# Two rows of a token block in one piece per partition, not four, in a fused gated-attention and MLP-mixer kernel

## The chip, the cores and the metric

The kernel runs on one core of a Trainium2 chip. A core has five engines with queues of their own: TensorE (PE; PEld is its weight loads), VectorE (DVE), ScalarE (ACT), GpSimd (POOL) and SyncE (SP). Work moves between the on-chip memories SBUF and PSUM, and DMA engines bring data from DRAM and transpose it. POOL, SP and ACT issue DMAs. Each engine works through its queue in order and waits on semaphores where an operand is not ready.

The metric is the device time of one execution in microseconds (us). The kernel before took 1173.21 us, the median of four runs (1169.92 to 1176.64).

## The reference

```python
# u, v: (8, 3008, 256)   z: (8, 3008, 64)   all float32
scores = (1 / S) * np.matmul(z, z.transpose(0, 2, 1))        # S = 3008
attn   = np.maximum(scores, 0.0) ** 2
x      = u * np.matmul(attn, v)
xt     = x.transpose(0, 2, 1)
h      = np.maximum(xt @ w_tok1, 0.0) @ w_tok2               # mixes tokens: 3008 -> 256 -> 3008
y      = x + h.transpose(0, 2, 1)
h2     = np.maximum(y @ w_ch1, 0.0) @ w_ch2                  # mixes channels: 256 -> 1536 -> 256
out    = y + h2
```

Every batch is independent of the others. The attention matrix of a batch is symmetric, because queries and keys are the same z.

## The kernel before, in words

Tokens are cut into 24 tiles of 128 (the last holds 64), four tiles to a block of 512: six query blocks (`q`, `NQ` = 6) and six key groups (`g`, `NG` = 6) per batch. Within a block the rows are dealt out to partitions: `rows_of` gives partition p four consecutive rows (4p to 4p+3), so a load moves one piece of four rows for each partition, and tile t of the block holds rows 4p + t. Attention does not mind in which order tokens come, as long as every operand has the same one. The last block holds three full tiles and a half one and is dealt three rows at a time.

**Attention.** `score_run` makes scores for two key tiles at a time. z has 64 channels, so a tile's z takes half of PE's rows; `zT` holds z transposed, doubled in both halves, and two score matmuls run side by side on the halves. PE changes between this mode and 128-row matmuls many times. ScalarE takes ReLU into an `at` buffer (six of them), VectorE squares it (L445), and PE multiplies it with v into two accumulators `acc0`, `acc1` (L533). From batch 1 on, a block above the diagonal is also transposed by SP's DMA queue (`flip`, L492) into an `fl` buffer and used again below the diagonal; the diagonal block itself is made as a triangle (L485). When a query block is complete, `gate` (L628) multiplies the two accumulators by `uT`, the transposed u block, into `xT`, and `turn_x` (L640) transposes that on SP.

**Mixer.** A batch's mixer runs between the attention steps of the next batch. `tok1` (L675) adds up over all six blocks; `tok2` (L692) makes h for one block, and VectorE adds it onto `xT` (L698); `ch1` (L729), an evacuation on ScalarE or VectorE (L742, L744), `ch2` (L771), and a residual add (L784) follow, and SP writes the output rows.

**z and its turns.** For batch 0 z is read as float32 on SP and ACT. Blocks 0 and 1 are doubled on VectorE and turned by PE matmuls with an identity, blocks 2 and 3 by DMA, blocks 4 and 5 by PE inside the attention loop (`turn_late_z`). For later batches POOL loads a `zs` buffer (`load_z`), copies it twice into `zr` (L125; two buffers), and SP transposes `zr` into `zT` (L126), one block at a time.

**Loads.** All loads but the first z are asked for by POOL, which casts to bf16 on the way. POOL also reorders w_tok2: `load_w_tok2` brings a piece into a `ws` buffer, and `order_w_tok2` (L220, L224) copies it into the order in which the tiles hold the tokens. A load waits where its buffer is still in use: u has three `ur` buffers, freed by `turn_u` (L189) on SP.

**The order.** The order of all queues is written by a planner at build time, in plain Python: it keeps a modelled time for each engine (`free`, `pe`), a list of waiting operations with a cost and a latency each (`push`), and a ring of three PSUM slots of two banks (`ring`; tag `ps`), which scores, token-mix, channel-mix and output pieces share. At every step the main loop picks scores, a half of an AV group or a mixer piece, by what the model says is ready. A `Piece` is a mixer step. Loads and turns are hung on attention steps by number (`at_group`), and take their place in POOL's or SP's queue when PE's planned order reaches that step. `release`, `live` and `ROOM` count buffers.

Of the kernel before, what the change touches and what calls it, by code (L numbers as in the profile page):

```python
# [13 lines left out]
P = 128  # L14
# [30 lines left out]
class Piece:  # L45


    def __init__(self, cost, needs, fn, opens=False, closes=False, room=None):
        self.cost, self.needs, self.fn = cost, needs, fn
        self.opens, self.closes, self.room = opens, closes, room  # L50


@with_exitstack
def kernel(
# [23 lines left out]
    NG = KT // GK  # L78
    widths = [min(QW, S - q * QW) for q in range(NQ)]
# [15 lines left out]


# [5 lines left out]
    def rows_of(ap, c):  # L102

        n = full_tiles[c]
        return ap[c * QW:c * QW + n * P, :].rearrange("(p t) d -> p t d", t=n)
# [4 lines left out]
    def load_z(b, c):  # L110
        zs = sb.tile([P, GK, d_qk], BF16, tag="zs", name="zs", bufs=6)
        n = full_tiles[c]
        nc.gpsimd.dma_start(out=zs[:, :n, :], in_=rows_of(z[b], c))
        if n < GK:
            for r in range(2):
                nc.gpsimd.dma_start(
                    out=zs[r * TAIL:(r + 1) * TAIL, n, :], in_=last_rows(z[b]))
        loading(LOAD / 4)
        return zs

    def turn_z(zs, zT, c, engine, tag="zr", bufs=2):


        zr = sb.tile([P, GK, 2, d_qk], BF16, tag=tag, name="zr", bufs=bufs)
        engine.tensor_copy(zr[:], zs.unsqueeze(2).to_broadcast([P, GK, 2, d_qk]))  # L125
        nc.sync.dma_start_transpose(  # L126
            out=zT[:, c * GK:c * GK + GK, :], in_=zr.rearrange("p t h d -> p (t h d)"))

    def first_z(c):
# [4 lines left out]
        queues[c % 2].dma_start(out=zf[:, :n, :], in_=rows_of(z[0], c))  # L134
# [25 lines left out]
    def load_v(b, c):  # L160
# [7 lines left out]
        nc.gpsimd.dma_start(out=vt[:, :n, :], in_=rows_of(v[b], c))  # L168
# [7 lines left out]
    def load_u(b, q):  # L176
        ur = sb.tile([P, QW // P, D], BF16, tag="ur", name="ur", bufs=3)
        n = full_tiles[q]
        nc.gpsimd.dma_start(out=ur[:, :n, :], in_=rows_of(u[b], q))
# [15 lines left out]
    def load_w_tok1(c):  # L195
        n = full_tiles[c]
        nc.gpsimd.dma_start(
            out=w_tok1_sb[:, c * GK:c * GK + n, :], in_=rows_of(moe_w_tok1, c))
# [6 lines left out]
    def load_w_tok2(c):  # L205
        st = sb.tile([P, DT, QW], BF16, tag="h2", name="ws", bufs=ROOM["h2"])
        W = widths[c]
        nc.gpsimd.dma_start(
            out=st[:, :, :W],
            in_=moe_w_tok2.rearrange("(tc t) s -> t tc s", t=P)[:, :, c * QW:c * QW + W])  # L210
        ws[c] = st
        live["h2"] += 1
        loading(LOAD)

    def order_w_tok2(c):
        st = ws.pop(c)
        live["h2"] -= 1
        W, n = widths[c], full_tiles[c]
        for h in range(DT):
            nc.gpsimd.tensor_copy(  # L220
                w_tok2_sb[:, h, c * QW:c * QW + n * P].rearrange("p (t s) -> p t s", s=P),
                st[:, h, :n * P].rearrange("p (s t) -> p t s", t=n))
        if n * P < W:
            nc.gpsimd.tensor_copy(  # L224
                w_tok2_sb[:, :, c * QW + n * P:c * QW + W], st[:, :, n * P:W])

# [15 lines left out]
    zTs, vs, urs, uTs, xTs, xs, ws = {}, {}, {}, {}, {}, {}, {}  # L242
# [9 lines left out]

    LAST = NG - 1

# [40 lines left out]

    LOAD = 1.3
# [84 lines left out]
    def score_run(us, start):  # L381
        slots = sorted((d for d in ring if d.t is not None), key=lambda d: d.t)
        for unit in us:
# [12 lines left out]
            for r, i, c0, c1 in parts(unit):  # L396
                k = g * GK + i
                h = slice(r * d_qk, (r + 1) * d_qk)
                nc.tensor.matmul(  # L399
                    sc[:, r, c0:c1], zT[h, k * P:(k + 1) * P],  # L400
                    zT[h, q * QW + c0:q * QW + c1], start=True, stop=True)
# [41 lines left out]
    def square(unit, view, t):  # L443
# [15 lines left out]
        if flips(b, q, g):  # L459
            uses[0] = 2  # L460
            attn = at.rearrange("p (j i s) -> p i j s", i=GK, s=P)
            done = push("sp", t, 2.45, 6.5, lambda t: flip(b, q, g, at, uses, done),
# [5 lines left out]
    def square_triangle(unit, t):  # L468
# [5 lines left out]
        if pr == 0:  # L474
            for j, busy in ((0, 0.55), (1, 0.4)):
# [3 lines left out]
        done = push("sp", t, 0.3, 5.5, lambda t: blocks.update(  # L479
# [136 lines left out]
    def gate(blk, dh, t):  # L616
# [18 lines left out]
        if dh == DT - 1:  # L635
            push("sp", t, 1.25, 7.5, lambda t: turn_x(b, q, t), first=1)
# [22 lines left out]
    def add_mixer(b):  # L659
# [26 lines left out]
        def tok2(q, end):  # L686
# [9 lines left out]
            def add(t):  # L696
                xT = xTs[b, q]
# [413 lines left out]
```

## Time and profile before

| | |
|---|---|
| median of four runs | 1173.21 us (1169.92 to 1176.64) |
| profiled execution, its own time | 1172.68 us |
| span of the profiled execution | 1170.8 us |
| TensorE | 1159.8 us busy, 7049 matmuls |
| VectorE, ScalarE, GpSimd | 541.3, 521.4, 158.9 us busy |
| share of the 16 DMA engines: SP's queue, POOL's queue | 53.6%, 19.9% |
| DMA packets | 472883, of them 27344 on POOL's queue (32.32 MB) |
| POOL copies: z doubling (L125), w_tok2 order (L220) | 42 of 631 ns; 12 of 522 to 816 ns |
| add after the token mix (L698), 1024 elements | 40 of 1214 ns |

How to read it: a group's busy time is the sum of its instructions' durations, and consecutive ones overlap at their ends, so PE's busy time is more than the time in which it streams columns. Idle time ahead of an instruction is put down to what was ready last. In a timeline line, the first number is the start, the second the length of the merged group, x the count, and the square bracket holds the idle time before it and what ended it. DMA shares are averages over all 16 engines. Rows of 40 digits give the busy share of 40 equal slices in tenths.

### The profile page before, as it was taken

To read this page: it belongs to the slowest core of one execution; us is meant where nothing else is said; L and a number is where in the kernel's file an instruction comes from. 1 tells how busy PE (TensorE), PEld (TensorE's weight loads), DVE (VectorE), ACT (ScalarE), POOL (GpSimd) and SP (SyncE) were. 2 spreads that over 40 slices of the span, in tenths; PEclk is the share of its full clock that TensorE was granted. 3 is DMA by queue.
4 is the path that set the end of the run, shared out by engine and by line. 5 is a ranking of instruction groups with operands and counts; after the bars stand their busy time and mean duration, and the time that the engine had idled before them with its cause. 6 is when DMAs were issued, how large, how long until landed. Compare 5 with 4: busy or idle time off the path is not lost.

```text
span 1170.8 us, 17791 instructions
## 1 busy us (share of the span) xinstructions
PE 1159.8 (99%) x7049; PEld 629.8 (54%) x7049; DVE 541.3 (46%) x819; ACT 521.4 (45%) x650; POOL 158.9 (14%) x328
## 2 busy tenths in 40 slices
PE   9999999999999999999999999999999999999998
PEld 3334554655546555555555655465454655555666
DVE  5785653356432554335634355242542336512544
ACT  7876543344542364343534435344454344513221
POOL 3372001102012100120101210101201000000000
PEclk9999999999999999999999999999999999999999
DMA  9999837797487975896759985698667977532121
GB/s 167 171 162 192 176 97 151 155 190 126 119 168 150 168 140 126 158 169 148 142 129 172 159 159 122 136 189 149 122 142 142 188 143 154 121 97 61 50 81 64
DMA packets 472883, 165.57 MB, mean 141 GB/s; under 512 B 436640, under 2 KB 450528, under 8 KB 472800
## 3 DMA queue, kind: packets, MB, share of 16 engines
q1 hardware_dynamic: 444944, 131.74, 53.6%
q0 software_dynamic: 27344, 32.32, 19.9%
q8 instruction: 55, 0.90, 0.3%
q10 hardware_dynamic: 512, 0.38, 0.1%
q14 instruction: 28, 0.23, 0.1%
HBM read 65.40 MB, written 24.64 MB: 77 GB/s over the span
## 4 chain that ended last, share of the span: by engine, by line
PE 95%; DVE 1%; DMA 1%; ACT 1%; issue 1%; SPq 0%; POOL 0%; ACTq 0%; DVEq 0%
PE acc L533 41%; PE op L771 21%; PE hp L729 21%; PE sc L399 6%; PE a_ps L675 4%; PE h_ps L692 3%; ACT at L437 1%; DVE at L445 1%; DMA zf<-in_z_dram 1%; DMA fl<-at 1%; DMA v_sb<-in_v_dram 0%; DVE xT L698 0%; DVE xT L628 0%; DVE h2pre L744 0%; SPq L134 0%
## 5 line engine op out<-in xcount | busy, mean ns | idle before, releaser
L533 PE MATMUL acc<-at,v_sb 128*128 128x512 bf16 (+3 forms) x1464 | 350.7, 378 | 3.5 <-DVE xT L628 2.7
L533 PEld LDWEIGHTS <-v_sb 128*128 128x128 bf16 (+1 forms) x2304 | 209.4, 97 | 269.0 <-issue 66.9
L742 ACT ACTIVATE h2pre<-hp 128x1024 bf16<-128x1024 f32 (+1 forms) x191 | 191.0, 1006 | 364.5 <-PE hp L729 363.4
L437 ACT ACTIVATE at<-sc 128x1024 bf16<-128x1024 f32 (+1 forms) x284 | 272.0, 1024 | 161.6 <-PE sc L399 156.1
L445 DVE TENSOR_TENSOR at<-at 128x1024 bf16<-128x1024 bf16 (+1 forms) x284 | 200.1, 713 | 177.2 <-ACT at L437 176.7
L729 PE MATMUL hp<-xT,w_ch_sb 128*128 128x512 bf16 (+1 forms) x1152 | 266.8, 375 | 0.0
L771 PE MATMUL op<-w_ch_sb,h2pre 128*128 128x256 bf16 x2208 | 258.4, 273 | 0.3 <-DVE xT L698 0.2
L771 PEld LDWEIGHTS <-h2pre 128*128 128x128 bf16 x2208 | 215.9, 98 | 46.2 <-issue 0.5
L533 PE MATMUL acc<-fl,v_sb 128*128 128x512 bf16 (+1 forms) x840 | 199.9, 371 | 0.0
L729 PEld LDWEIGHTS <-w_ch_sb 128*128 128x128 bf16 x1152 | 112.7, 98 | 126.7 <-issue 0.2
L784 DVE TENSOR_TENSOR res<-op,u_sb 128x512 f32<-128x512 f32 x87 | 60.1, 691 | 206.5 <-PE op L771 206.5
L744 DVE TENSOR_SCALAR h2pre<-hp 128x1024 bf16<-128x1024 f32 (+1 forms) x97 | 117.3, 1209 | 52.4 <-PE hp L729 51.5
L628 DVE TENSOR_TENSOR xT<-acc,uT 128x512 bf16<-128x512 f32 (+1 forms) x96 | 63.2, 665 | 113.8 <-PE acc L533 113.6
L399 PE MATMUL sc<-zT 64*128 64x512 bf16 (+1 forms) x732 | 95.0, 360 | 0.3
L425 ACT ACTIVATE at<-sc 128x512 bf16<-128x512 f32 (+3 forms) x164 | 59.2, 446 | 67.7 <-PE sc L399 67.5
L125 POOL COPY zr<-zs 128x512 bf16<-128x512 bf16 x42 | 26.5, 631 | 400.3 <-DMA zT<-zr 394.4
L473 DVE TENSOR_TENSOR at<-at 128x512 bf16<-128x512 bf16 (+3 forms) x164 | 44.4, 324 | 59.2 <-ACT at L425 59.1
L399 PEld LDWEIGHTS <-zT 64*128 64x128 bf16 x732 | 31.3, 94 | 56.8 <-issue 39.4
L698 DVE TENSOR_TENSOR xT<-xT,h_ps 128x1024 bf16<-128x1024 bf16 (+1 forms) x48 | 55.7, 1192 | 6.4 <-PE h_ps L692 6.3
L168 POOL DMA_DIRECT2D v_sb<-in_v_dram x48 | 25.9, 545 | 145.2 <-PE acc L533 144.3
L675 PE MATMUL a_ps<-x_sb,w_tok_sb 128*128 128x256 bf16 x384 | 44.7, 273 | 0.8 <-ACT at L437 0.8
L692 PE MATMUL h_ps<-w_tok_sb,a_sb 128*128 128x512 bf16 (+1 forms) x192 | 44.5, 375 | 0.1
(43 smaller groups left out, 210.0 us busy)
## 6 DMA issues: line engine op xcount, KB each, us to landing
out_dram<-res SPq DMA_DIRECT2D x87, 256.0 KB, 2.2
v_sb<-in_v_dram POOLq DMA_DIRECT2D x40, 256.0 KB, 4.8
ur<-in_u_dram POOLq DMA_DIRECT2D x40, 256.0 KB, 5.1
zs<-in_z_dram POOLq DMA_DIRECT2D x35, 64.0 KB, 4.6
at<-at SPq DMA_TRANSPOSE x123, 2.4
fl<-at SPq DMA_TRANSPOSE x105, 4.0
v_sb<-in_v_dram POOLq DMA_DIRECT2D x8, 192.0 KB, 6.1
ur<-in_u_dram POOLq DMA_DIRECT2D x8, 192.0 KB, 5.5
```

What stands on the lines that cost most here:

```text
L399: nc.tensor.matmul(sc[:, r, c0:c1], zT[h, k * P:(k + 1) * P], zT[h, q * QW + c0:q * QW + c1], start=True, stop=True)
L437: nc.scalar.activation(view, sv, ACT.Relu, scale=inv_S)
L445: nc.vector.tensor_mul(view, view, view)
L533: nc.tensor.matmul(o, vs[blk.b, g][rows, i, dh * P:(dh + 1) * P], rhs, start=first, stop=stop, skip_group_check=True)
L628: nc.vector.tensor_mul(xT[:, dh, :full * P].rearrange("p (t s) -> p t s", s=P), acc[:, :full * P].rearrange("p (t s) -> p t s", s=P), uT[: ...
L675: nc.tensor.matmul(st["a_ps"][:, th, :], w_tok1_sb[:, k, th * P:(th + 1) * P], x[:, :, i, :], start=(k == 0 and th == 0), stop=(k == KT - ...
L692: nc.tensor.matmul(h[:, dh, :W], st["a"][:, th, dh * P:(dh + 1) * P], w_tok2_sb[:, th, q * QW:q * QW + W], start=(th == 0), stop=(th == 1))
L729: nc.tensor.matmul(hp[:, r, :W], w_ch1_sb[:, dc, cc * P:(cc + 1) * P], xT[:, dc, :W], start=(dc == 0), stop=(dc == DT - 1))
L742: nc.scalar.activation(h2[:, :, :W], hp[:, :, :W], ACT.Relu)
L744: nc.vector.tensor_single_scalar(h2[:, :, :W], hp[:, :, :W], 0.0, AX.max)
L771: nc.tensor.matmul(op[:, i, :], h2, w_ch2_sb[:, cc, :], start=(cc == 0 and (i == 0 or apart)), stop=(cc == CHT - 1), skip_group_check=True)
L784: nc.vector.tensor_add(res.rearrange("p i (h d) -> p i h d", d=P), op.rearrange("p i (h d) -> p i h d", d=P), us[:, :, half * 2:half * 2 + ...
```

## The change

The token order. In a full block a partition now holds two pieces of two consecutive rows: tile 2a + t holds rows 256a + 2p + t. `fetch_rows` loads both pieces with one DMA, `out_rows` writes one half of a block as one run of two rows per partition. The last block stays dealt by three.

Along with that:

- w_tok2 is loaded straight into its place in its natural column order (no `ws` buffer, no copies on POOL). The add after the token mix takes h from PSUM at a step of two elements, in two instructions per full block.
- z of batches 1 to 7 goes into one standing tile `zs` with a slot of zeros at either end. One transpose turns pairs of neighbouring tiles: with two transposes shifted by one tile against each other, slot k of `zT` holds tile k-1 in its lower and tile k in its upper rows. So nothing is doubled on POOL; the two halves of a score matmul read slots k+1 and k (`z_tile`). Five transposes per batch, two of six tiles for each half of the batch and one of a single tile.
- z blocks 4 and 5 of batch 0 and the first u block are turned on PE as mixer pieces marked `urgent`; u(0,0) no longer uses a DMA transpose. Its evacuation from PSUM is a VectorE copy of 1024 elements.
- In batch 0 `turn_x` waits until the planned time 62 us; z of batch 1 is loaded from the seventh attention step on, not the nineteenth, and turned in two halves.
- In the planner, a flip costs 1.8 us of SP's time in place of 2.45, each transpose of a triangle 1.2 in place of 0.55, 0.4 and 0.3, and scores may be held back (`together`) until the half tile at the end of the keys can go with them in the same PE mode.

```diff
+    zs = consts.tile([P, KT + 2, d_qk], BF16)
-    def rows_of(ap, c):
-        n = full_tiles[c]
-        return ap[c * QW:c * QW + n * P, :].rearrange("(p t) d -> p t d", t=n)
+    def fetch_rows(queue, to, ap, c):
+        n = full_tiles[c]
+        rows = ap[c * QW:c * QW + n * P, :]
+        if n == GK:
+            queue.dma_start(
+                out=to.rearrange("p (a t) d -> p a t d", a=2),
+                in_=rows.rearrange("(a p t) d -> p a t d", a=2, t=2))
+        else:
+            queue.dma_start(out=to, in_=rows.rearrange("(p t) d -> p t d", t=n))
+    def out_rows(b, q, half):
+        if full_tiles[q] == GK:
+            rows = out[b][q * QW + half * 2 * P:q * QW + (half + 1) * 2 * P, :]
+            return rows.rearrange("(p t) d -> p t d", t=2)
...
-    def turn_z(zs, zT, c, engine, tag="zr", bufs=2):
-        zr = sb.tile([P, GK, 2, d_qk], BF16, tag=tag, name="zr", bufs=bufs)
-        engine.tensor_copy(zr[:], zs.unsqueeze(2).to_broadcast([P, GK, 2, d_qk]))
-        nc.sync.dma_start_transpose(
-            out=zT[:, c * GK:c * GK + GK, :], in_=zr.rearrange("p t h d -> p (t h d)"))
+    def turn_z(zT, half):
+        n = KT // 2
+        for k in (half * n, half * n + 1):
+            nc.sync.dma_start_transpose(
+                out=zT[:, k:k + n:2, :],
+                in_=zs[:, k:k + n, :].rearrange("p t d -> p (t d)"))
+        if half:
+            nc.sync.dma_start_transpose(
+                out=zT[:, KT, :], in_=zs[:, KT:, :].rearrange("p t d -> p (t d)"))
...
     def load_w_tok2(c):
-        st = sb.tile([P, DT, QW], BF16, tag="h2", name="ws", bufs=ROOM["h2"])
+        cols = slice(c * QW, c * QW + widths[c])
         nc.gpsimd.dma_start(
-            out=st[:, :, :W],
-            in_=moe_w_tok2.rearrange("(tc t) s -> t tc s", t=P)[:, :, c * QW:c * QW + W])
+            out=w_tok2_sb[:, :, cols],
+            in_=moe_w_tok2.rearrange("(tc t) s -> t tc s", t=P)[:, :, cols])
-    def order_w_tok2(c):
...
-            done = push("sp", t, 2.45, 6.5, lambda t: flip(b, q, g, at, uses, done),
+            done = push("sp", t, 1.8, 6.5, lambda t: flip(b, q, g, at, uses, done),
...
-            push("sp", t, 1.25, 7.5, lambda t: turn_x(b, q, t), first=1)
+            push("sp", t if b else max(t, LOADED), 1.25, 7.5,
+                 lambda t: turn_x(b, q, t), first=1)
...
             def add(t):
                 xT = xTs[b, q]
-                nc.vector.tensor_add(xT[:, :, :W], xT[:, :, :W], h[:, :, :W])
+                n = full_tiles[q]
+                if n == GK:
+                    to = xT.rearrange("p h (a t s) -> p h a t s", a=2, t=2)
+                    own = h.rearrange("p h (a s t) -> p h a t s", a=2, t=2)
+                    for half in range(2):
+                        nc.vector.tensor_add(
+                            to[:, :, half], to[:, :, half], own[:, :, half])
+                else:
+                    to = xT[:, :, :n * P].rearrange("p h (t s) -> p h t s", t=n)
+                    nc.vector.tensor_add(
+                        to, to, h[:, :, :n * P].rearrange("p h (s t) -> p h t s", t=n))
...
+            at_group(base + NG, lambda b=b: new_zT(b + 1))
             for j, c in enumerate(vorder):
+                ask = base + (NG if b == 0 else 3 * NG - 2)
+                at_group(ask + j, lambda b=b, j=j: load_z(b + 1, j))
+                if j % 3 == 2:
+                    at_group(ask + (2 * j + 4 if b == 0 else j + 3),
+                             lambda b=b, j=j: turn_next_z(b, j // 3))
...
+    def first_u(landed):
+        ur = urs.pop((0, 0))
+        def turn(end):
+            take_slot()
+            up = psum.tile([P, QW // P * DT, P], F32, tag="ps", name="up", bufs=3)
+            for i in range(QW // P * DT):
+                t, h = divmod(i, DT)
+                nc.tensor.matmul(
+                    up[:, i, :], ur[:, t, h * P:(h + 1) * P], ident[:],
+                    start=(i % 4 == 0), stop=True, skip_group_check=True)
+            ring.append(push("dve", end + 0.2, 1.15, 1.3, lambda t: evacuate(up)))
...
+        heads.append(Piece(0.45, [Done(landed)], turn, urgent=True))
...
+    late_z(4, 7.8)
+    late_z(5, 9.0)
+    first_u(18.5)
...
+        together = (
+            blk is not None and blk.q > 1 and blk.b < B - 1 and not blk.tails
+            and blk.slot == 0 and t + 0.3 < tails_ready(blk) < FAR)
+        if n_now and not together and ts <= t + NOW and (whole or (low and n_now >= 2)):
             pick = "scores"
...
+        elif tm <= t + NOW and pieces[0].urgent:
+            pick = "mixer"
```

## The prediction, made before the result was known

> **What bounds the kernel now.** I read the page's busy table and the rows by slice first, then the chain, then the timeline around each place where TensorE stood idle.
>
> ```profile
> PE 1159.8 (99%) x7049; PEld 629.8 (54%) x7049; DVE 541.3 (46%) x819; ACT 521.4 (45%) x650; POOL 158.9 (14%) x328
> ...
> PEclk9999999999999999999999999999999999999999
> DMA  9999837797487975896759985698667977532121
> ...
> PE 95%; DVE 1%; DMA 1%; ACT 1%; issue 1%; SPq 0%; POOL 0%; ACTq 0%; DVEq 0%
> ```
>
> TensorE is the bound at full granted clock, and the chain is TensorE for 95%. A busy PE row overstates matmuls, so I redid it by rate: in the chain 12 AV matmuls of 512 columns take 2.59 us (0.216 each) and 48 of 256 columns 5.24 us (0.109). All matmuls at these rates (scores two at a time, as they run on two row halves) come to 1135 us of the 1170.8 us span. The other 36 us are: about 23 us in 254 changes between 64-row scores and 128-row matmuls (0.09 each, counted in PE's order), about 6 before and after the first and last matmul, and the rest in a few holes, all before 111 us but one. From 120 to 1080 us no 20 us stretch lost more than 0.2 us apart from the changes. So a gain can come from the holes alone, and they are these.
>
> ```profile
> 71.51 9.65 DVE L445 TENSOR_TENSOR at<-at 128x1024 bf16<-128x1024 bf16 x8 [0.76 <-ACT at L437]
> ...
> 74.35 1.91 POOL L220 COPY w_tok_sb<-ws 128x512 bf16<-128x512 bf16 x2
> ...
> 81.81 2.43 PE L533 MATMUL acc<-at,v_sb 128*128 128x448 bf16 x12 [1.29 <-DVE xT L628]
> ```
>
> Eight squares take 9.65 us, 1.2 apiece, while POOL reorders w_tok2 (L220); at 94 us four took 2.55, 0.64 apiece. The gate is late, and PE waits 1.29 us.
>
> ```profile
> 98.60 0.53 POOL L179 DMA_DIRECT2D ur<-in_u_dram  x1 [12.47 <-DMA uT<-ur]
> 99.12 1.08 POOL L113 DMA_DIRECT2D zs<-in_z_dram  x2
> 100.18 8.01 SPq L492 DMA_TRANSPOSE fl<-at  x3
> ...
> 106.29 2.85 ACT L437 ACTIVATE at<-sc 128x1024 bf16<-128x1024 f32 x3 [4.41 <-DMA fl<-at]
> 107.37 1.03 PE L675 MATMUL a_ps<-x_sb,w_tok_sb 128*128 128x256 bf16 x8 [0.80 <-ACT at L437]
> ...
> 109.61 0.37 PE L533 MATMUL acc<-at,v_sb 64*128 64x512 bf16 x1 [1.21 <-DVE xT L628]
> ```
>
> Batch 1's first flips (the transposed copies fl) queue behind late loads; ScalarE cannot overwrite at for 4.41 us, and PE loses 0.80 + 1.21 + 0.22 us.
>
> ```profile
> 11.80 1.04 PE L533 MATMUL acc<-at,v_sb 128*128 128x512 bf16 x4 [0.48 <-DMA v_sb<-in_v_dram]
> ...
> 1094.44 5.52 PE L692 MATMUL h_ps<-w_tok_sb,a_sb 128*128 128x512 bf16 x24
> 1095.51 6.74 DVE L698 TENSOR_TENSOR xT<-xT,h_ps 128x1024 bf16<-128x1024 bf16 x6 [0.46 <-PE h_ps L692]
> 1100.17 3.00 PE L771 MATMUL op<-w_ch_sb,h2pre 128*128 128x256 bf16 x26 [0.21 <-DVE xT L698]
> ```
>
> At 11.8 us PE waits for the second v block. At 1095 us six token-mix pieces outrun six adds (1.12 us apart); three PSUM slots hold them up by 0.64 us in all.
>
> **The change, part by part.**
>
> 1. **w_tok2 reorder and z doubling leave POOL.** 13 copies (L220/L224, 0.5 to 0.8 us) and 42 (L125, 0.63) go; nothing waits for POOL instead, and w_tok2 lands in its place. Squares fall back from 1.2 to 0.64 us, so the wait at 81.8 goes: bounds -1.4 and 0 (if ScalarE, at 0.92 us a pair, were late next). I take **-1.3**.
>
> 2. **Loads earlier, four x turns later.** POOL was held by z copies waiting for z turns (8.3 us at 60), so the w_tok2 and w_ch loads came at 61 to 85 and were still running at 93. Now POOL's queue is v, u, z, w without these waits; batch 0's x turns are moved on SP behind the u and z turns to 62 us and are needed only at about 106. SP's next uses are u turns needed at each gate, 10 us or more later. What is late next is the fifth u load and the four flips themselves (1.4 to 1.7 us issue each at best), so ScalarE may still wait a little. Bounds -2.7 (whole hole) and 0; I take **-2.2**, near the hole's shown 2.23.
>
> 3. **Two rows in one piece.** v, u and w_tok1 loads go from 128 pieces of 4 KB to 256 of 2 KB, z from 1 KB to 512 B. The trace's packet records on POOL's queue have 173 ns (median) for 2048 bytes written and 98 for 1024: two halves cost 196, +13%. Hidden from 24 us on (loads are asked for long before use), but not at the start: z of batch 0 and v share full DMA engines there. zf 4 releases POOL at 7.78 us and would come some 0.5 later; POOL's issue goes from 0.545 us (128 pieces) towards 0.705 (L208, 256 pieces); the second v block lands some 0.8 later, on PE's path. Output stores keep 2 KB pieces. Against it, casts and turns of z 4, z 5 (waits of 0.17 to 0.67 us at 10.9 and 15.4) are now placed by the planner, and u(0,0) is turned on PE. That sits behind the load in PE's own queue, with AV matmuls and scores behind it; but u(0,0) landed by 18.1 us, and the eight matmuls come at about 22.5, so it hides. Bounds -0.9 (waits of 0.48, 0.17, 0.28 go) and +1.5 (zf and v both late, with the z turns behind them); I take **+0.4**.
>
> The DMA page of the Trainium skill ("DMA: Bandwidth & Descriptors", § Why small descriptors are slow) gives a fixed cost of about 3 bus cycles a packet beside 32-byte beats. By that, halving 4 KB would cost an estimated 2%, and the start would lose almost nothing; the packet records say 13%, and I go by them.
>
> 4. **PE instructions.** Eight more matmuls of 128 columns at 0.056 us (128/512 of 0.216, plus a little), +0.45; PE's order has 252 changes in place of 254, -0.18: **+0.26**. The z turns are 25 tiles per batch in five issues, not 24 in six: nothing on PE's path.
>
> 5. **The add after the token mix** reads PSUM at a step of two floats, as two instructions of 512 for one of 1024. Two unstepped 512-element operations follow each other at 0.61 to 0.64 us (gates L628: two in 1.27 to 1.29), so 1.22 against 1.12. At 1095 us PE's order in the changed kernel puts six pieces, two ch1 pieces (moved ahead of op), then op; at 0.1 us more an add and with two more slots to wait for, the stops sum to 0.24+0.36+0.46+0.46+0.35 = 1.87 us against 0.64: **+1.2**. Elsewhere the pieces stand among AV work (three, then gaps of 0.86 to 1.7 us): 42 adds by 0.1 us, mostly covered by those AV matmuls; without the cover, +4. I take **+0.4**, bounds 0 and +4. No row reads PSUM at a step. Upper end: half rate, which adds 0.53 us per 512 elements (the slope between 691 ns for 512 and 1214 for 1024), 2.27 us an add. Lower end: no slower than 1.12, if the two halves overlap better, giving -0.6 at 1095 us. I take the unstepped rows, the nearest in kind.
>
> The PSUM page ("PSUM — Partial Sum Buffer", § Specifications) speaks against this: lines of 8 bytes, and "any non-contiguous AP slows matmuls significantly". It says so of matmuls, not of a VectorE read; if it held for the add, each element would touch its own line, and the sum would go to the first rival's. No row of this trace shows it.
>
> Sum: -1.3 - 2.2 + 0.4 + 0.26 + 1.2 + 0.4 = **-1.2 us**, against the profiled execution's 1172.68 us (span 1170.8, 1.9 around it), 0.53 below the median of the four runs, 1173.21. So 1172.0 against that median, within what a measurement of this kernel can tell from no change (0.5%, 5.9 us).
>
> **Rivals.**
>
> *A, slower: the stepped PSUM read runs at half rate.* 2.27 us an add. At 1095 us the last six take 13.6 us, not 6.7: about +7. In seven other batches six adds take 6.9 us longer on VectorE, with squares and evacuations behind them; VectorE is 46% busy, so I let half of it reach PE: +24. These 31 us in place of item 5's 1.6 give +28, about **1201**. With x us an add it costs (21+7)(x-1.12) against gains of 2.8 in items 1 to 4: slower by 0.5% from x = 1.43. For it: three slots, and PE at 99%. Against it: one element a cycle is already the rate here.
>
> *B, the loads do not clear.* Finer pieces keep the DMA engines full (they are at 9 in most early slices) and flips still meet u loads: item 2 gives nothing, item 3 +1.5: -1.3+1.5+0.26+1.2+0.4 = +2.1, **1175**. For it: 13% more packet time. Against it: loads start about 10 us earlier.
>
> *C, all holes close.* -1.4-2.7-0.9+0.26, and the adds hide (+0.3): -4.4, **1168.8**. For it: the planner's flip and triangle times are now nearer the rows (1.8 and 1.2 us). Against it: the three-slot stop at 1095.
>
> **How the numbers follow.** Forecast 0.46, C 0.22, B 0.18, A 0.14. The forecast's own spread is about 1169 to 1175. The range takes in C with a run's scatter (the four runs span 1169.9 to 1176.6), B, and the near part of A (1.5 us an add, +8): 1166.5 to 1181, leaving 0.06 below and 0.12 above. Faster by over 0.5% needs under 1167.3, more than the known holes hold: half of C and a lucky scatter, 0.13. Slower needs over 1179.1: A, and a tail of B, 0.19. Same 0.68.
>
> **What will show it.** Right: no PE wait at 82 or 105 to 111 us, squares at 0.64 throughout batch 0, w_ch loads done before 65 us; adds of 0.69 us a half; a longer stop before the last op group; the first PE waits for v 0.5 to 1 us later. Wrong: adds over 0.9 us a half; PE waiting on u(0,0) or z turns; holes in batches 1 to 6.

## The result, and the profile after

The changed kernel took 1184.28 us, the median of 35 runs, against 1171.75 for the kernel before in 54 runs. The ratio on record is 1.0085, 95% interval 1.0068 to 1.0101; the quotient of the two medians is 1.0107. The changed kernel is slower by about 1%, where 1172.0 and no measurable change had been forecast. The median lies above the forecast's range of 1166.5 to 1181 too. All ratios on record leave out runs that lie more than 1.5% above the fastest of their kernel (the one of 3827 us here, three runs each of e1 and e8, and one of before in each of two series), so they can be nearer to 1, or lower, than the medians.

The times are not spread around one value. Of the 35 runs, 29 took 1177.5 to 1189.4 us, five took 1172.2 to 1176.6, and one 3827. The kernel before does the same the other way round: 48 of 54 took 1169.8 to 1176.6, six 1179.8 to 1186.8. The profiles below show a stop of TensorE whose size differs from run to run. Below, a time over 1177 us counts as a run with a large stop. For runs without a profile this is inferred, but their mean granted clock fits it: in after's profile the clock is low around the stop and in the last 2 us alone, and its mean is 0.994; among the 31 runs of before made beside e1 it is 0.993 to 0.997 in the five over 1177 us and 0.998 or more in the others. Kernels are compared only with runs of before that were made in the same series, because that share varies between series (5 of 31, 12 of 31, 9 of 31 and 2 of 19 runs of before).

The profiled execution of after took 1182.89 us (span 1181.1), 10.2 more than that of before. Its page, first the busy table, then the clock and the DMA engines by slice, then the chain:

```profile
PE 1160.9 (98%) x7057; PEld 630.4 (53%) x7057; DVE 557.2 (47%) x882; ACT 509.1 (43%) x636; POOL 149.9 (13%) x275
...
PEclk9997999999999999999999999999999999999999
DMA  9999866888768987696987797677797957443121
...
PE 97%; DMA 1%; DVE 1%; SPq 1%; issue 0%; ACT 0%; POOL 0%; ACTq 0%
```

TensorE is still the bound, and its busy time differs by 1.1 us from before. Only one digit tells: the clock row shows 7 in the fourth slice, 89 to 118 us. TensorE stood still there. The waits between 90 and 120 us (who waited for whom: total, times, longest) name it:

```profile
ACT at L456 <- DMA fl<-at: 12.7, 1, 12.7
PE sc L418 <- ACT at L456: 12.5, 1, 12.5
```

It is the same wait as the 4.41 us of ScalarE that the prediction showed at 106 us in before: ScalarE cannot overwrite an `at` buffer until a flip has read it. In before it cost TensorE 2.2 us, here 12.5. SP's queue in the timeline (start, length of the merged group, count):

```profile
70.41 22.87 SPq L661 DMA_TRANSPOSE x_sb<-xT  x4
93.38 4.07 SPq L224 DMA_TRANSPOSE uT<-ur  x1
97.54 1.26 SPq L661 DMA_TRANSPOSE x_sb<-xT  x1
98.89 1.26 SPq L224 DMA_TRANSPOSE uT<-ur  x1
100.24 3.90 SPq L511 DMA_TRANSPOSE fl<-at  x1
104.24 1.64 SPq L661 DMA_TRANSPOSE x_sb<-xT  x1
105.97 10.71 SPq L511 DMA_TRANSPOSE fl<-at  x4
```

The first line is the four x turns held to 62 us. They were to take 1.25 us each; they take 5.7, while POOL's loads are still being written. The u turns come behind them, at 93 and 99 us, the first flip at 100.24 (93.13 in before), and the last four at 106 to 116.7. ScalarE's wait ends when the second flip has landed: at 113.1 us, and at 106.2 in before. POOL, ScalarE and TensorE at that time:

```profile
100.09 0.71 POOL L114 DMA_DIRECT2D ur<-in_u_dram  x1 [13.59 <-DMA uT<-ur]
102.25 0.71 POOL L114 DMA_DIRECT2D ur<-in_u_dram  x1 [1.44 <-DMA uT<-ur]
102.96 2.88 POOL L114 DMA_DIRECT2D zs<-in_z_dram  x4
113.17 3.77 ACT L456 ACTIVATE at<-sc 128x1024 bf16<-128x1024 f32 x4 [12.66 <-DMA fl<-at]
114.25 0.61 PE L418 MATMUL sc<-zT 64*128 64x512 bf16 x2 [12.51 <-ACT at L456]
```

POOL waited 13.59 us for a late u turn to free a `ur` buffer, and so asks for two u blocks and four z blocks at 100 to 106 us, amid the flips (before asked for one u block and four z blocks at 98.6 to 101.2). It goes in a circle: turns are late for loads, and loads are late for turns.

I counted TensorE's loss per stretch as in the prediction: its time, less matmuls at full rate, less 0.09 us for each change of row mode. From before to after it goes from 2.77 to 14.50 us at 100 to 120 us, from 1.15 to nothing at 80 to 100, from 5.3 to 5.0 in the first 40 us, and from 0.7 to 1.5 at 1080 to 1120. The first of these, +11.7, is more than the whole 10.3 us of span.

### The profile page after: what moved, and what is told of

Its sections match the earlier page's. It is cut to its first block, busy times and chain, and to the rows that moved or that the text cites. A ratio compares the mean times of both kernels' runs of the same rounds, so it can differ in the third digit from the quotient of the medians.

```text
span 1181.1 us, 17803 instructions
## 1 busy us (share of the span) xinstructions
PE 1160.9 (98%) x7057; PEld 630.4 (53%) x7057; DVE 557.2 (47%) x882; ACT 509.1 (43%) x636; POOL 149.9 (13%) x275
## 4 chain that ended last, share of the span: by engine, by line
PE 97%; DMA 1%; DVE 1%; SPq 1%; issue 0%; ACT 0%; POOL 0%; ACTq 0%
PE acc L552 42%; PE op L806 21%; PE hp L764 21%; PE sc L418 7%; PE a_ps L696 4%; PE h_ps L713 3%; DMA fl<-at 1%; DMA zf<-in_z_dram 1%; DVE xT L725 0%; DMA v_sb<-in_v_dram 0%; SPq L511 0%; SPq L661 0%; DVE h2pre L779 0%; DVE at L492 0%; ACT at L456 0%
## 5 line engine op out<-in xcount | busy, mean ns | idle before, releaser
L552 PE MATMUL acc<-at,v_sb 128*128 128x512 bf16 (+2 forms) x1464 | 351.2, 379 | 1.8 <-DMA v_sb<-in_v_dram 1.2
L777 ACT ACTIVATE h2pre<-hp 128x1024 bf16<-128x1024 f32 (+1 forms) x177 | 177.8, 1007 | 314.3 <-PE hp L764 312.3
L464 DVE TENSOR_TENSOR at<-at 128x1024 bf16<-128x1024 bf16 (+1 forms) x284 | 194.7, 688 | 198.6 <-ACT at L456 198.0
L764 PE MATMUL hp<-xT,w_ch_sb 128*128 128x512 bf16 (+1 forms) x1152 | 263.9, 375 | 0.5 <-DVE xT L725 0.5
L552 PE MATMUL acc<-fl,v_sb 128*128 128x512 bf16 (+1 forms) x840 | 196.2, 371 | 0.0
L779 DVE TENSOR_SCALAR h2pre<-hp 128x1024 bf16<-128x1024 f32 (+1 forms) x111 | 133.6, 1204 | 58.9 <-PE hp L764 58.8
L418 PE MATMUL sc<-zT 64*128 64x512 bf16 (+1 forms) x732 | 94.8, 360 | 12.5 <-ACT at L456 12.5
L114 POOL DMA_DIRECT2D v_sb<-in_v_dram x40 | 29.3, 735 | 421.7 <-PE acc L552 421.3
L725 DVE TENSOR_TENSOR xT<-xT,h_ps 128x512 bf16<-128x512 bf16 x80 | 49.6, 680 | 0.6 <-PE h_ps L713 0.6
L114 POOL DMA_DIRECT2D ur<-in_u_dram x40 | 28.8, 721 | 139.8 <-DMA uT<-ur 126.5
```

Source lines behind the costliest of these rows:

```text
L418: nc.tensor.matmul(sc[:, r, c0:c1], zT[h, k:k + P], zT[h, m + c0:m + c1], start=True, stop=True)
L464: nc.vector.tensor_mul(view, view, view)
L552: nc.tensor.matmul(o, vs[blk.b, g][rows, i, dh * P:(dh + 1) * P], rhs, start=first, stop=stop, skip_group_check=True)
L764: nc.tensor.matmul(hp[:, r, :W], w_ch1_sb[:, dc, cc * P:(cc + 1) * P], xT[:, dc, :W], start=(dc == 0), stop=(dc == DT - 1))
L777: nc.scalar.activation(h2[:, :, :W], hp[:, :, :W], ACT.Relu)
L779: nc.vector.tensor_single_scalar(h2[:, :, :W], hp[:, :, :W], 0.0, AX.max)
```

## The experiments

One theory, **D**, came from this: the DMA engines are full from 2 us to about 115 us, in before too (by stretches of 13 to 22 us their share is 0.97 to 1.33 in before and 0.93 to 1.38 in after; it passes 1 where packets overlap). Whatever is added or pushed back reaches the flips of 93 to 113 us, which no mixer work covers: PE's first token-mix matmul of after is at 116 us. Its rivals: **F**, the finer pieces alone; **X**, the held x turns alone, through the order of SP's queue; **C**, the DMA engines stall by chance, whatever is asked of them. (These letters are not those of the prediction's rivals.) A narrower form of D, here **U**, has no run of its own: that the u and z blocks asked for amid the flips make them late, and not what was loaded before. All kernels were timed ten times.

| kernel | median us | range | over 1177 us | before in that series |
|---|---|---|---|---|
| e1: after, rows by four | 1182.56 | 1168.6 to 1196.1 | 7 of 10 | 5 of 31 |
| e2: after, x turns not held | 1171.45 | 1167.8 to 1185.0 | 4 of 10 | 5 of 31 |
| e3: before, x turns held | 1172.48 | 1170.9 to 1175.6 | 0 of 10 | 5 of 31 |
| e4: before, rows by two | 1176.8 | 1171.7 to 1185.7 | 5 of 10 | 5 of 31 |
| e5: after, w_ch amid the flips | 1176.34 | 1174.4 to 1177.9 | 4 of 10 | 12 of 31 |
| e6: e5, x turns not held | 1176.26 | 1175.8 to 1177.3 | 1 of 10 | 12 of 31 |
| e7: before, w_ch amid the flips | 1179.6 | 1178.3 to 1184.4 | 10 of 10 | 12 of 31 |
| e8: after, rows by four, x not held | 1173.18 | 1167.9 to 1195.6 | 4 of 10 | 12 of 31 |
| e9: after, w_ch behind the flips | 1168.63 | 1168.0 to 1172.0 | 0 of 10 | 9 of 31 |
| e10: e9, x turns not held | 1169.47 | 1168.0 to 1172.8 | 0 of 10 | 9 of 31 |
| e11: e10, w_ch 21 us later | 1177.87 | 1177.4 to 1179.0 | 10 of 10 | 9 of 31 |
| e12: before, w_ch behind the flips | 1169.1 | 1168.6 to 1170.6 | 0 of 10 | 9 of 31 |
| e14: e8, z as in before | 1169.1 | 1167.8 to 1176.5 | 0 of 10 | 2 of 19 |
| e15: e4, w_ch behind the flips | 1169.42 | 1168.9 to 1170.7 | 0 of 10 | 2 of 19 |

### One part taken back, or done alone

**e1, rows by four in the changed kernel.** Loads and stores deal four rows to a partition as in before, and the add reads PSUM at a step of four elements in one instruction.

```diff
-        if n == GK:
-            queue.dma_start(
-                out=to.rearrange("p (a t) d -> p a t d", a=2),
-                in_=rows.rearrange("(a p t) d -> p a t d", a=2, t=2))
-        else:
-            queue.dma_start(out=to, in_=rows.rearrange("(p t) d -> p t d", t=n))
+        queue.dma_start(out=to, in_=rows.rearrange("(p t) d -> p t d", t=n))
...
-                    to = xT.rearrange("p h (a t s) -> p h a t s", a=2, t=2)
...
+                to = xT[:, :, :n * P].rearrange("p h (t s) -> p h t s", t=n)
+                nc.vector.tensor_add(
+                    to, to, h[:, :, :n * P].rearrange("p h (s t) -> p h t s", t=n))
```

> The changed kernel with the token order put back to four rows in one piece (loads, stores, and the add after the token mix, which then reads PSUM at a step of four floats in one instruction of 1024); all else stays. Theory F (the finer pieces slow POOL's loads, so they still run at 92 us and the first flips meet them): the 12.5 us wait of PE for scores at 102 us goes or falls under 4 us, POOL's loads of w_ch end before 80 us, time 1170 to 1174 us. Theory X (the four x turns of batch 0 that are held to 62 us fill SP's queue in the load stretch, and the flips stand behind them on SP): the wait stays at 9 to 13 us, SP still takes 15 to 25 us for those four turns, time 1180 to 1186. Under both, the add's duration tells what the step costs: 1.2 us if nothing, 2.2 us at half rate; at half rate the three-slot stop near 1105 us grows from 1.2 to about 8 us.

Measured: median 1182.56, seven of ten over 1177; ratio 1.003, 95% interval 0.9989 to 1.0072. Its profile is of a run at 1173.16, with a small stop. SP's queue, and the wait at the flips:

```profile
70.65 13.87 SPq L653 DMA_TRANSPOSE x_sb<-xT  x4
...
94.53 12.69 SPq L503 DMA_TRANSPOSE fl<-at  x4
```

```profile
PE sc L410 <- ACT at L448: 3.3, 1, 3.3
```

The held turns still take 3.5 us each and the four flips 3.2, though the pieces are as large as before. The wait of 3.3 us is what F expected, but it is that of a run with a small stop; the median and the seven of ten are X's. F alone falls.

**e2, x turns not held.** One constant:

```diff
-    LOADED = 62.0
+    LOADED = 0.0
```

> The changed kernel with the x turns of batch 0 put into SP's queue as soon as each gate is done (planned time 0 in place of 62 us); two rows in one piece stay. Theory X: each x turn is issued by itself in some 1.3 us, the first flip starts at 92 to 95 us, not 100, the 12.5 us wait shrinks to 0 to 3 us, and the time is 1168 to 1172 us, at or below the kernel before. Theory F: the loads still end at 90 us or later, flips still land in 6 to 9 us, the wait stays above 6 us, and the time is 1178 to 1184.

Measured: median 1171.45, ratio 1.0006 (0.997 to 1.0042); four of ten over 1177, the other six at 1167.8 to 1172.9. The median is X's, but the share of large stops fell only from 29 of 34 for the changed kernel (another series) to four of ten, and the profile (a run at 1179.46) has the same wait:

```profile
PE sc L418 <- ACT at L456: 7.6, 1, 7.6
```

That wait is F's. The held turns are a large part, and not all. The four fastest runs, at 1167.8 to 1169.2, lie under all 31 of before in that series (1169.9 and up).

**e3, the x turns held in the kernel before.**

```diff
-            push("sp", t, 1.25, 7.5, lambda t: turn_x(b, q, t), first=1)
+            push("sp", t if b else max(t, 62.0), 1.25, 7.5,
+                 lambda t: turn_x(b, q, t), first=1)
```

> The kernel before with one thing of the change: the x turns of batch 0 held to the planned time 62 us. Theory X: its loads too run to 93 us, so SP is blocked the same way, the first flips come 5 us or more later than at 93 us, and it is 6 to 14 us slower than the kernel before (1178 to 1186). Theory F: within 2 us of the kernel before.

Measured: median 1172.48, ratio 0.999 (0.9964 to 1.0017), none of ten over 1177. The hold does no harm in the kernel before, so X falls as a cause by itself. Why it does none is not shown: the planner's order shifts with the hold (POOL asks for w_ch at 71 to 81 us, not 77 to 85), so this run is not the hold alone.

**e4, rows by two in the kernel before.** Loads and stores as in the changed kernel; POOL's w_tok2 copies write the new order, so the add has no step.

```diff
+        if n == GK:
+            queue.dma_start(
+                out=to.rearrange("p (a t) d -> p a t d", a=2),
+                in_=rows.rearrange("(a p t) d -> p a t d", a=2, t=2))
...
+                nc.gpsimd.tensor_copy(
+                    w_tok2_sb[:, h, c * QW:c * QW + n * P].rearrange(
+                        "p (a t s) -> p a t s", a=2, t=2),
+                    st[:, h, :n * P].rearrange("p (a s t) -> p a t s", a=2, t=2))
```

> The kernel before with the token order alone changed: two rows in one piece for loads and stores, and POOL's reordering of w_tok2 made for that order; z doubling, x turns and the add stay as before. Theory F: POOL's loads take 10% more DMA time, end later than 93 us, and the hole at 105 to 111 us grows from 2.2 us to 8 us or more, 1178 to 1184 us. Theory X: no more than 3 us slower (the start 0.5 us, the hole 1 to 2 us more), 1172 to 1175.

Measured: median 1176.8, ratio 1.003 (0.9997 to 1.0063); five of ten at 1179.9 to 1185.7, the others at 1171.7 to 1173.7. This lies between the two expectations. The finer pieces leave the five lower times where before's median is (1172.31 in that series), and the large stop comes in half of the runs, not in a sixth, a difference that is near what chance gives in ten runs. Both suspects so seem to act on how often the large stop comes, and neither explains it alone, which fits D.

### The load on the DMA engines moved

The next kernels leave all suspects in place, and take 1.57 MB of loads out of the crowded time: the channel-mix weights w_ch, which POOL asks for at 59 to 71 us and PE first uses at 140. Every engine but POOL keeps its order. POOL works in order, so one u block and four z blocks (0.52 MB) that stand behind w_ch on its queue move with it.

**e5, e6, e7.** POOL waits for a flip, with a one-column copy of it, and then asks:

```diff
+    late_w_ch = lambda part: (part or nc.gpsimd.tensor_copy(mark[:, :1], blocks[1, LAST, 0][1][:, 0, :1]), load_w_ch(part))
     def ask_w_ch(part):
-        load_w_ch(part)
+        at_group(NQ * NG + 9, lambda: late_w_ch(part)); loading(LOAD * 1.5)
```

> The changed kernel, with the four channel-mix weight loads (1.57 MB as stored) asked of POOL only when the last flip of the batch's first 512 tokens has landed, some 105 us, and not at 59 to 70 us; they are first used at 140 us. Every other instruction keeps its order. Theory D (the DMA engines are full from 2 us on; work carried over 93 us makes the flips of 93 to 115 us land late, ScalarE finds no free buffer and TensorE waits): the loads end before 85 us, the wait of 12.5 us shrinks to under 3, the median falls from 1182.6 to 1168 to 1172, at most two of ten times are over 1178. Rival S (the flips are late for the order of SP's own queue, the bunch of x turns before them, whatever the loads do): the wait stays at 8 to 13 us, seven or eight of ten times are over 1178, median 1180 to 1184.

> The same late channel-mix weights, and the x turns not held to 62 us. Theory D: no wait over 2 us at the flips in any run, 1167 to 1169 in at least nine of ten, against four of ten at 1178 to 1185 with the loads where they were: the fastest of all so far. Rival S: as without the late loads, median 1171, three to five of ten at 1178 to 1185, since the part of SP's queue is already out of it.

> The kernel before, with the channel-mix weights asked after the last flip of the batch's first 512 tokens, and not at 77 to 85 us. Theory D: its own wait at 105 to 111 us (2.7 us) goes, and with it the one time in six over 1178: 1168 to 1171 in all ten. Rival S: 1172, one or two of ten over 1178, as before.

Measured: 1176.34, 1176.26 and 1179.6, ratios 1.0007 (0.998 to 1.0034), 0.9993 (0.9972 to 1.0014) and 1.0022 (0.9998 to 1.0046). No expectation held, by a mistake of mine: the block chosen, that of the last key group, is the one that is flipped first, not last. So the weights were asked amid the flips. SP's and POOL's lines of e5:

```profile
95.63 22.82 SPq L511 DMA_TRANSPOSE fl<-at  x4
...
96.43 0.18 POOL L1020 CAST mark<-fl 128x1 f32<-128x1 bf16 x1 [5.84 <-DMA fl<-at]
96.66 1.10 POOL L248 DMA_DIRECT2D w_ch_sb<-in_moe_w_ch_dram  x2
97.74 1.69 POOL L253 DMA_DIRECT2D w_ch_sb<-in_moe_w_ch_dram  x2
```

The mistake is the clearest dose of all. With 1.57 MB among them, and the u and z blocks behind it, four flips take 22.8 us, and TensorE loses 8.35 us at 100 to 120 us (7.7 in e6, 6.0 in e7; the profiles from e5 on lack 93 matmul records each, which adds some 0.4 us to such a count). By the times it does so in every run: none of the 30 is under 1174.3, the range of e6 is 1.5 us where that of e2 was 17, and e5 and e6, with the x turns held or not, have the same median. The rival S of these expectations, by which the loads do not matter, falls.

**e9, e10, e12.** The same with the wait on the fifth and last flip:

```diff
-    late_w_ch = lambda part: (part or nc.gpsimd.tensor_copy(mark[:, :1], blocks[1, LAST, 0][1][:, 0, :1]), load_w_ch(part))
+    late_w_ch = lambda part: (part or nc.gpsimd.tensor_copy(mark[:, :1], [blocks[k][1] for k in blocks if k[0] == 1 and k[2] == 0 and k[1] > k[2] and blocks[k][2] == 'fl'][-1][:, 0, :1]), load_w_ch(part))
```

> As the first kernel with late weights, but POOL's wait is on the fifth and last flip of the batch's first 512 tokens; there it was on the first, which sent 1.57 MB among the other four (22.8 us for four, TensorE idle 8 us, in every run). Held x turns, two rows. Theory D: the four flips take 8 us or less, TensorE idles under 2 us at 95 to 115 us, 1167 to 1171 in at least eight of ten. Theory C (chance stalls of the DMA engines make the wait, whatever is asked): three or more of ten over 1177 as without it.

> As the run above with the x turns not held to 62 us. Theory D: 1166.5 to 1169 in at least nine of ten, at least 3 us under the kernel before. Theory C: three to five of ten over 1177, as when only the turns were not held.

> The kernel before with the weights asked after the last of the first 512 tokens' flips (POOL's wait on the last that the order has by then). Theory D: its wait of 2.7 us at 105 to 111 us goes and no time is over 1177: 1168 to 1171 in all ten. Theory C: 1172, one or two of ten over 1178, as before.

Measured: 1168.63, 1169.47 and 1169.1 us; ratios to before 0.9953 (0.9928 to 0.9978), 0.9965 (0.9943 to 0.9988) and 0.9959 (0.9936 to 0.9982). None of the 30 runs is over 1172.8, against nine of 31 of before over 1177. SP's and POOL's lines of e9, which has the held turns and the finer pieces:

```profile
91.24 3.93 SPq L511 DMA_TRANSPOSE fl<-at  x1
95.27 1.25 SPq L661 DMA_TRANSPOSE x_sb<-xT  x1
96.62 7.87 SPq L511 DMA_TRANSPOSE fl<-at  x4
...
106.47 0.18 POOL L1020 CAST mark<-fl 128x1 f32<-128x1 bf16 x1 [15.11 <-DMA fl<-at]
106.70 1.10 POOL L248 DMA_DIRECT2D w_ch_sb<-in_moe_w_ch_dram  x2
107.78 1.69 POOL L253 DMA_DIRECT2D w_ch_sb<-in_moe_w_ch_dram  x2
```

The four flips take 7.9 us and not 22.8, and TensorE's loss at 100 to 120 us is 0.3 us. The four held x turns take 12.5 us (22.9 in after), and the second flip has landed at 100.5 us (113.1 in after). D's expectations for e9 and e12 held. C falls: what is asked of the engines decides whether large stops come. e10 was expected within 1169 in nine of ten and has four there, so that not holding the turns adds nothing once there is room. e12 shows that the kernel before paid for the same crowding: freed of it, it gains 3.0 us. The three rows below are of before, e12 and e9, from the table of busy time by stretch (PE's busy time is the second number; the last three are the granted clock, the DMA share and GB/s; 80 to 93 us):

```profile
80.00:93.00 13.00, 11.71 (x71) 5.05 (x68) 9.37 (x15) 9.57 (x11) 6.13 (x11) 1.00 1.16 175
```

```profile
80.00:93.00 13.00, 12.95 (x75) 5.45 (x75) 8.87 (x17) 11.10 (x13) 1.32 (x4) 1.00 0.55 97
```

```profile
80.00:93.00 13.00, 12.96 (x75) 5.24 (x75) 9.42 (x18) 11.78 (x14) 1.43 (x2) 1.00 1.22 164
```

In e12 the DMA share just before the flips is halved, from 1.16 to 0.55, and PE is busy for all of the 13 us. POOL's queue moved 1.96 MB there in before and 0.64 in e12. In e9 the share is not lower: it is 1.22, against 1.31 in after. But SP's own transposes fill it, and POOL's queue moved 0.30 MB there, against 1.55 in after. So a full DMA row does not by itself make the flips late. What tells all sixteen profiles apart is what POOL's queue writes amid the first flips, at 93 to 105 us: 0.33 to 1.06 MB in before, after and e1 to e7, while SP's transposes move 1.09 to 1.77 MB; 0.25 MB at most in the others, where SP's move 2.47 to 2.96. The DMA share is 1.08 to 1.35 in the first group and 1.07 to 1.19 in the second.

These bytes fit U as well as D, and no run decides between the two. In the profiles of before, after and e1 to e4, which lose 2.8 to 14.5 us at 100 to 120 us, POOL asks for a u block and four z blocks at 92 to 106 us. In e9, e10, e12 and e15 these wait behind w_ch until 107 us or later, and in the profiles of e8 and e14 below, which lose at most 1 us there, they came at 88 to 91. No run moves them and leaves the rest.

**e11, later still.** e10 with the wait on a flip of the second 512 tokens (the last but one was meant):

```diff
-    late_w_ch = ... [blocks[k][1] for k in blocks if k[0] == 1 and k[2] == 0 and ...
+    late_w_ch = ... [blocks[k][1] for k in blocks if k[0] == 1 and k[2] == 1 and ...
...
-        at_group(NQ * NG + 9, lambda: late_w_ch(part)); loading(LOAD * 1.5)
+        at_group(NQ * NG + 10, lambda: late_w_ch(part)); loading(LOAD * 1.5)
```

> As the run above, with POOL's wait on the last flip but one of the second 512 tokens, some 10 us later (about 115 us; first use at 140 us). If the loads still meet flips that count at 105 to 115 us in the run above, this one is 1 to 3 us faster and its times lie closer together; if they do not, both are the same within 1 us; if the weights come too late, TensorE waits for them at 140 us and this one is slower by that wait.

Measured: 1177.87 us, all ten within 1.6 us, ratio 1.0021 (0.9991 to 1.0051). POOL's line and TensorE's wait:

```profile
125.47 0.18 POOL L1020 CAST mark<-fl 128x1 f32<-128x1 bf16 x1 [47.50 <-DMA fl<-at]
```

```profile
PE hp L764 <- DMA w_ch_sb<-in_moe_w_ch_dram: 7.5, 2, 4.6
```

The third expectation came true. The flip waited for is the fourth and last of these tokens in SP's queue; it landed at 125, not 115 us, and the weights were too late by 7.5 us. At 106 us (e9) nothing waited for them, so an estimate from the two puts the end of the good place at some 118 us.

### What the rest of the change adds

**e8, e14.** e8 takes back both suspects in the changed kernel (the edits of e1 and e2). e14 also asks and turns batch 1's z at the steps of before:

```diff
-                ask = base + (NG if b == 0 else 3 * NG - 2)
+                ask = base + 3 * NG - 2
...
-                    at_group(ask + (2 * j + 4 if b == 0 else j + 3),
+                    at_group(ask + j + 3,
```

> The changed kernel with the order of four rows in one piece and the x turns not held: both suspected parts taken back, while the z loads and turns, the weights in plain order and the start stay as changed. If the finer pieces and the held turns are all of it: 1167 to 1170, at most one of ten over 1177. If the rest of the change (z asked and turned earlier in batch 0, without POOL's copies to slow the loads) also crowds the engines: 1170 to 1174, three or more of ten over 1177.

> The changed kernel with the order of four rows, the x turns not held, and the next batch's z rows asked and turned at the gates of before also in batch 0: with rows and turns alone taken back, four of ten were over 1177. If the earlier z loads are what is left of the crowding: 1167.5 to 1170, at most one of ten over 1177. If it is POOL, which no longer stops for its copies and asks the weights some 14 us earlier, so that they and the turns meet: three or more of ten over 1177, median 1170 to 1175.

Measured: e8 has four of ten under 1169.3 and four over 1177, three of them at 1191.7 to 1195.6; before had 12 of 31 over 1177 in that series, so e8's share is that of before, though its three longest times are over all of before's (1188.6 at most). e14 has none over 1177 (median 1169.1, ratio 0.9984, 0.9964 to 1.0004), against two of 19 of before. So with rows and turns taken back these few runs show no larger share of large stops than before, but whether the z loads matter is not settled by ten runs against ten. The profiled runs of both lose nothing at 100 to 120 us worth naming (0.13 and 0.95 us) and have another stop, at the start of batch 4. This is e14's:

```profile
599.16 0.98 ACT L436 ACTIVATE at<-sc 128x512 bf16<-128x512 f32 x2 [4.08 <-DMA fl<-at]
...
600.19 1.87 PE L749 MATMUL hp<-xT,w_ch_sb 128*128 128x512 bf16 x4 [3.11 <-ACT at L436]
```

It is the same wait at another batch's first flips. Why it comes in these two and not in e9 or e12 is open. What made e8's three slowest runs was not seen, as none of them was profiled.

**e15, the price of the finer pieces alone.** e4 with w_ch behind the flips, by the edit of e12.

> The kernel before with the order of two rows, and the channel-mix weights asked after the flips: against the same with four rows (1169.1, all within 1168.6 to 1170.6) it prices the finer pieces where the crowding is gone. Theory D (they cost only by crowding): 1168.5 to 1170.5 in at least nine of ten. If they cost by themselves as the prediction summed them (0.4 us at the start, 1.2 us at the stepped add): 1170 to 1171.5. If they alone fill the engines again: three or more of ten over 1177.

Measured: 1169.42 us, 1168.9 to 1170.7, ratio 0.9967 (0.9946 to 0.9989). Against e12 (1169.1, another series) that is 0.3 us, inside the scatter. The finer pieces cost nothing measurable where w_ch and what follows it stand behind the flips; what price they have is in the crowding.

## Why the prediction was wrong

The forecast took 2.2 us off for a hole that in truth grew by 11.7. **Item 2 failed**, in two of its statements and in the sign that was drawn from it. "Loads earlier" was right for asking, not for landing: the w_ch loads were asked at 59 to 71 us, and not at 77 to 85, but in 60 to 84 us a w_ch load took 19.3 us to land, and POOL's queue still moved 1.55 MB in 80 to 93 us (1.96 in before). The last of them landed at 91.4 us, against 95.1 in before, so that "w_ch loads done before 65 us" was wrong by 26 us. Having the last load asked 13 us earlier moved its landing by under 4. The DMA row shown of before has a 9 in each of its first four slices, 0 to 117 us, but item 3 read it only for the start, and only rival B for the rest. "Needed only at about 106" priced the held turns by who reads their result. The cost lay in who stands behind them on SP, the u turns and flips, and in what they share the engines with: a 256-byte transpose packet took 52 ns on average in 60 to 93 us, against 25 in before, by the packet records. The step also named what would be late next, "the fifth u load and the four flips themselves", and then gave it a little, where it was all of the loss.

**Item 3's size was right and its cover wrong.** "Hidden from 24 us on" holds for a load that is asked early on engines with room. Here 13% more packet time, by the prediction's packet records, is taken from a queue that ends at the flips: in e4 five of ten runs had a large stop, in before 5 of 31, and e15 showed no cost without the crowding. The start itself, put at +0.4, came out at about -0.35 together with the other changes there; in e4's profile, with the finer pieces alone, the first 40 us lose 7.7 us, against 5.3 in before.

**Rival B had the mechanism, and a fifth of the price.** It said that the engines stay full and flips meet u loads, at 1175 us. It kept the hole at its old size, as if the 2.23 us shown were the most that the place could lose. That size varies from run to run: the times of before go up to 1186.8, some 15 us over the usual, though none of its runs with a large stop was profiled.

**The other steps held.** Item 1: TensorE's wait at 82 us is gone, and its loss at 80 to 100 us fell by 1.2 us, where -1.3 was given; single squares take 0.69 us. (In e12 the wait is gone as well, with POOL's copies in place and ten squares at 1.03 us apiece, so that the copies were not its only condition.) Item 4 is as counted. Item 5 was too dear. The lines of after around 1103 us, and the group of the adds:

```profile
1103.95 6.07 DVE L725 TENSOR_TENSOR xT<-xT,h_ps 128x512 bf16<-128x512 bf16 x10 [0.46 <-PE h_ps L713]
1107.68 0.93 PE L713 MATMUL h_ps<-w_tok_sb,a_sb 128*128 128x448 bf16 x4 [0.16 <-DVE xT L725]
1108.88 0.93 PE L764 MATMUL hp<-xT,w_ch_sb 128*128 128x448 bf16 x4 [0.27 <-DVE xT L725]
1110.08 0.93 PE L764 MATMUL hp<-xT,w_ch_sb 128*128 128x448 bf16 x4 [0.27 <-DVE xT L725]
```

```profile
L725 DVE TENSOR_TENSOR xT<-xT,h_ps 128x512 bf16<-128x512 bf16 x80 | 49.6, 680 | 0.6 <-PE h_ps L713 0.6
```

Ten half adds in 6.07 us are 1.21 a pair, as summed, but the stops come to 0.16 + 0.27 + 0.27 = 0.70 us, not 1.87. By the count of TensorE's loss at 1080 to 1120 us the place costs about 0.8 us more than in before, where +1.2 was given; the +0.4 given for the adds elsewhere is not seen: from 120 to 1080 us that count is near nothing in both kernels. **Rival A falls**: a half add at a step of two takes 680 ns, and in e1 a whole one at a step of four takes 1212 ns, against 1214 unstepped. The sentence of the Trainium skill's page "PSUM — Partial Sum Buffer" (§ Specifications) on non-contiguous patterns slowing matmuls does not extend to VectorE's read here.

**With the crowding out of both kernels, the change is worth little**: e9 against e12, in one series, 1168.63 against 1169.1, or -0.5 us, which is inside the scatter of ten runs. Items 1, 3, 4 and 5 summed to about +1.0, and to +2.3 without item 1, whose wait is gone from e12 too. So outside the place where the time is, the forecast was off by 1.5 to 3 us, little beside the 11.7; this does not confirm the sizes of these items one by one.

What is not settled: what decides from run to run how large the stop gets, and how the excess divides between the held turns, the pieces and the earlier z loads. That the large stop needs POOL's loads ahead of the flips or among them is shown: none of the 40 runs of e9, e10, e12 and e15, which moved them, is over 1172.8, against 11 of 50 of before over 1177 in the same two series. How much of this is w_ch (1.57 MB) and how much the u and z blocks that moved with it (0.52 MB) is not shown.

## What to carry to other kernels

When the loads ahead of it are still being written, a load asked 13 us earlier can land only 4 us earlier, as here, and a transfer with a late reader is not free to move: price it by what stands behind it on its queue and on the engines, at the first place where a transfer is needed at once. A wait of 2 us at such a place is a sample and not a size; look at the spread of the times before taking it as the bound. The remedy was not fewer or larger packets but moving 1.57 MB that nobody needed yet, and the 0.52 MB behind it on the queue, past the place: 0.3 to 0.5% faster than before, in either kernel, and the times of each kernel within 2 to 5 us.

## What was not expected of the hardware

- The issue of a transpose on SP is not a fixed price. An x turn or a flip issued in 1.2 to 1.6 us at a DMA share of 0.40 (e10, 80 to 93 us), flips in 2.0 us each at 1.15 with SP's own transposes alone (e10, 94 to 102 us), and x turns (after, 70 to 93 us) and flips (e5, 96 to 118 us) in 5.7 us each while POOL's loads ran.
- After TensorE's 12.5 us of idleness the granted clock was 0.50 in 114 to 117 us of after: the first four AV matmuls of 512 columns took 1.89 us, against 1.04 at 8.4 us, and the first eight token-mix matmuls 1.72 us, against 1.03 in before. By these two, an estimate, the stop cost some 1.5 us more than its length.
- A VectorE add that reads PSUM at a step of two or four elements costs what an unstepped one does: 680 ns for 512, 1212 for 1024.
